# A wider third projection block, 34-row pairs in the last MLP step, and a written order for all engines

## The chip, the cores and the metric

The kernel runs on one core of one Trainium2 chip. The metric is the device time of one execution in microseconds. Before the change the median of three runs is 414.59 us (414.57 to 415.31). The profiled execution took 415.18 us; its span, from the first to the last instruction in the trace, is 413.4 us, at a mean granted TensorE clock of 0.999.

Names: TensorE (PE) multiplies matrices, its weight loads (PEld) run beside its matmuls; VectorE (DVE), ScalarE (ACT) and GpSimd (POOL) work element by element; SyncE (SP) issues the DMAs from one queue, in order.

## The reference

```python
S, D, F = 2048, 512, 1376
def _A_ref(x, wqkv, wo):            # H = 32 heads of 16, W = 8, dil = 2
    q, k, v = split(x @ wqkv)
    # token p attends to p, p-2, ..., p-14; places before 0 are masked
    logits = jnp.einsum("bhsd,bhswd->bhsw", q, kg) * scale
    attn = _softmax(logits, axis=-1)
    o = jnp.einsum("bhsw,bhswd->bhsd", attn, vg)
    return o.transpose(...).reshape(B, S, D) @ wo
def _B_ref(x, w1, b1, w2, b2):
    y = _layernorm(x, axis=-1)
    h = _gelu(jnp.einsum("bsd,df->bsf", y, w1) + b1)
    return jnp.einsum("bsf,fd->bsd", h, w2) + b2

xn = _layernorm(x, axis=-1)
return x + _A_ref(xn, A_wqkv, A_wo) * _silu(_B_ref(xn, B_w1, B_b1, B_w2, B_b2))
```

## The kernel before

**Arithmetic.** Every matmul of size is done three times in float16: an operand is split into a high part and a low remainder, and high x high, high x low and low x high are added in one PSUM bank. With D = 512 as KT = 4 blocks of 128 rows, one output tile takes 12 matmuls. The scales that keep the parts in float16's range come from sums of squares of the weights, worked out at the start (`sumsq`, L421; the results are `qsc`, `hsc`, `zsc`, `osc`).

**Tiling.** The 2048 tokens stand in two halves `c` (even and odd tokens) of NI = 8 tiles of 128. The 32 heads are NHB = 4 head blocks of 8 heads. The eight units u = (c, hb) each take `qkv`, then `attention`. The MLP runs over four chunks `ch` of 512 tokens and NF = 11 blocks of F: ten of 128 and a last one of FL = 96.

**The projection.** `qkv(c, hb, u)` multiplies each token tile's yT by 384 columns of `wq` (q, k and v of 8 heads; L746), evacuates with a scale to `U[u % 2]` on ScalarE (L763) or VectorE (L759), and copies the rows that neighbouring partitions need by DMA (L771). The first projection tiles wait for `prep` of the weights on ScalarE: squares with a running sum (`scale_q`, L514), high parts (`prep_q`, L536), and casts of the transposed, normalised tokens (`y0`, L687).

**Attention** is element work on VectorE (L805 to L863) and GpSimd (L873, L883); its result `o` (L848) is transposed by DMA (L851) to `oT`.

**The MLP.** `mlp1(ch, f)` makes 128 rows of h for 512 tokens in 12 matmuls (L1016), then a gelu (L1033) and the high part (L1036) on ScalarE and the low part (L1038) on VectorE. For f = 10 only 96 rows exist. `mlp2(ch, f)` follows two steps later (LAG = 2): 12 matmuls (L1052) into four banks z, one for each token tile, that collect all 11 blocks. The last block's h is in `hlast`, 96 rows and one row for the bias, so its 12 matmuls contract 97 rows. Then a silu, and the result g goes to DRAM (`gd`) until the end.

**The end.** `wo_first` (half c = 0) and `wo_last` (half c = 1, L951) multiply oT by `wo`; for half 1 VectorE evacuates with the product by g (L993), x is added on VectorE (L1000) or GpSimd (L997), and SP issues the output (L1002).

**The order.** Every operation is noted with its engine, a cost, what it reads and writes, and a priority. `Plan.issue` (L222) is a list scheduler: at each step it takes, over all engines, the ready operation that can start first by its cost model (`place`, L187), with the priority among those of an engine, and the program is issued in that order. Buffers of a ring are given out in the same step.

## Time and profile before

| what | value |
|---|---|
| median of three runs | 414.59 us |
| profiled execution | 415.18 us |
| its span | 413.4 us |
| granted TensorE clock | 0.999 |
| matmuls in the trace | 2083 |
| DMA moved | 46.41 MB, mean 112 GB/s |

The span can be cut in four. The columns are the length, and then the busy time of TensorE, weight loads, VectorE, ScalarE and GpSimd with their instructions in brackets, the granted clock, the share of the DMA engines and GB/s:

```profile
0.00:20.00 20.00, 16.48 (x81) 10.39 (x82) 14.00 (x44) 10.65 (x20) 11.55 (x21) 1.00 0.92 344
20.00:50.00 30.00, 29.73 (x179) 17.11 (x177) 25.86 (x50) 28.00 (x53) 9.77 (x7) 1.00 0.70 200
50.00:393.00 343.00, 342.96 (x1739) 170.54 (x1737) 329.05 (x273) 183.47 (x282) 95.20 (x101) 1.00 0.32 91
393.00:413.40 20.40, 16.76 (x90) 8.58 (x88) 10.61 (x16) 0.00 (x0) 3.82 (x3) 0.98 0.35 117
```

A group of instructions is read like this: line and engine, operation, output <- inputs (buffer numbers left out), partitions x elements, xcount | busy time in us, mean ns of one | idle time of the engine just before them, and what ended it. In the timeline the first two numbers are the start and the length in us, and a bracket at the end names the idle time before and its releaser. A record of a matmul is longer than the distance to the next, because matmuls overlap in the pipeline.

### The profile page before, as it was taken

Reading aid. Unit: us, or ns where it says so; the run is one execution under the profiler, and the core shown is the slowest. Engines: PE = TensorE matmul, PEld = TensorE weight load, DVE = VectorE, ACT = ScalarE, POOL = GpSimd, SP = SyncE. Lnnn points to the kernel's source line nnn. Section 1 sums busy time; section 2 is a strip of 40 time slices with the busy share of each in tenths; the row PEclk is TensorE's granted clock in tenths of the full one; section 3 lists DMA queues with packets and bytes.
Section 4 is the critical chain, followed back from the end, with each engine's and each line's share of the span. In section 5 each row is a group of like instructions: output and inputs, shape, how many; then the busy total and the mean of one; then the engine's idle time right before and its main releaser. Section 6 shows DMA issues by size and latency. Waiting matters only on the chain.

```text
span 413.4 us, 5554 instructions
## 1 busy us (share of the span) xinstructions
PE 405.9 (98%) x2083; PEld 206.6 (50%) x2083; DVE 379.5 (92%) x379; ACT 222.1 (54%) x353; POOL 120.3 (29%) x131
## 2 busy tenths in 40 slices
PE   8799999999999999999999999999999999999996
PEld 5555544445654455445544554455455544444443
DVE  4996989998999999989998999999999998999954
ACT  4699899994549655843384252225212393263500
POOL 3834002004380425042504330434033404520021
PEclk9999999999999999999999999999999999999999
DMA  8958717030045137720172034223604244007133
GB/s 281 397 112 258 235 61 230 0 128 1 1 142 152 28 93 183 149 46 2 48 221 75 0 102 116 68 86 88 205 7 122 88 111 145 0 18 238 23 102 131
DMA packets 47211, 46.41 MB, mean 112 GB/s; under 512 B 31785, under 2 KB 32225, under 8 KB 46673
## 3 DMA queue, kind: packets, MB, share of 16 engines
q1 hardware_dynamic: 47184, 46.06, 37.6%
q8 instruction: 16, 0.26, 0.3%
q14 instruction: 11, 0.08, 0.1%
HBM read 24.06 MB, written 7.34 MB: 76 GB/s over the span
## 4 chain that ended last, share of the span: by engine, by line
PE 92%; ACT 3%; issue 1%; DVE 1%; POOL 1%; ACTq 0%
PE z L1052 28%; PE ps L1016 28%; PE ps L746 25%; PE ps L929 5%; PE ps L961 2%; PE z L961 2%; PE pl L746 1%; ACT w L421 1%; PE pl L961 1%; ACT f L673 1%; ACT yT L687 0%; ACT wq L536 0%; POOL wq L471 0%; POOL rb L635 0%; ACT prod L661 0%
## 5 line engine op out<-in xcount | busy, mean ns | idle before, releaser
L1016 PE MATMUL ps<-yT,w 128*128 128x512 f16 (+1 forms) x528 | 120.4, 379 | 0.0
L746 PE MATMUL ps<-wq,yT 128*128 128x384 f16 x708 | 117.0, 326 | 0.2 <-DVE U L759 0.2
L1052 PE MATMUL z<-w,h 128*128 128x512 f16 x480 | 110.4, 379 | 0.0
L746 PEld LDWEIGHTS <-yT 128*128 128x128 f16 x744 | 72.5, 98 | 49.2 <-issue 1.0
L1016 PEld LDWEIGHTS <-w 128*128 128x128 f16 (+1 forms) x528 | 52.8, 100 | 61.0
L805 DVE TENSOR_TENSOR prod<-U 128x2048 f32<-128x2048 f32 x32 | 73.2, 2286 | 2.2 <-POOL prod L883 0.7
L1052 PEld LDWEIGHTS <-h 128*128 128x128 f16 x480 | 46.6, 98 | 55.5 <-issue 0.3
L808 DVE TENSOR_REDUCE L<-prod 128x128 f32<-128x2048 f32 x32 | 73.0, 2281 | 0.4
L1033 ACT ACTIVATE ps<-ps,b1T,hsc 128x512 f32<-128x512 f32 (+1 forms) x44 | 32.9, 748 | 73.4 <-PE ps L1016 72.2
L863 DVE TENSOR_TENSOR prod<-pl,U 128x2048 f32<-128x2048 f32 x28 | 63.2, 2283 | 4.2 <-POOL prod L873 4.1
L763 ACT ACTIVATE U<-ps,cs 128x384 f32<-128x384 f32 x54 | 31.2, 580 | 65.2 <-PE ps L746 65.2
L873 POOL TENSOR_TENSOR prod<-prod,prod 128x2048 f32<-128x2048 f32 x7 | 31.7, 4531 | 113.8 <-DVE prod L863 99.6
L883 POOL TENSOR_TENSOR prod<-prod 128x1024 f32<-128x1024 f32 x14 | 32.9, 2349 | 0.0
L882 POOL COPY gate<-prod 1x1 f32<-1x1 f32 x21 | 5.5, 264 | 91.0 <-DVE prod L805 82.2
L1038 DVE SCALAR_TENSOR_TENSOR h<-ps,hsc,h 128x512 f16<-128x512 f32 x40 | 29.6, 741 | 1.7 <-ACT h L1036 1.4
L1036 ACT ACTIVATE h<-ps,hsc 128x512 f16<-128x512 f32 x40 | 27.3, 684 | 1.3 <-PE z L1052 0.4
L929 PE MATMUL ps<-wo,oT 128*128 128x512 f16 x96 | 21.7, 379 | 0.0
L858 DVE TENSOR_TENSOR prod<-prod,prod 128x2048 f32<-128x2048 f32 x9 | 20.5, 2282 | 0.0
L1033 ACT ACT_TABLE_LOAD x10 | 12.8, 1283 | 8.6 <-PE ps L1016 8.5
L883 POOL TENSOR_TENSOR prod<-prod,prod 128x1024 f32<-128x1024 f32 x7 | 16.4, 2347 | 0.0
L961 PEld LDWEIGHTS <-oT 128*128 128x128 f16 x108 | 10.6, 98 | 10.4
L929 PEld LDWEIGHTS <-oT 128*128 128x128 f16 x96 | 9.4, 98 | 11.2
(179 smaller groups left out, 377.8 us busy)
## 6 DMA issues: line engine op xcount, KB each, us to landing
f<-in_A_x_dram SPq DMA_DIRECT2D x31, 256.0 KB, 3.5
U<-U SPq DMA_DIRECT2D x16, 392.0 KB, 4.0
gd<-f SPq DMA_DIRECT2D x12, 256.0 KB, 3.4
prod<-in_A_x_dram SPq DMA_DIRECT2D x8, 256.0 KB, 6.9
oT<-in_B_w_dram SPq DMA_DIRECT2D x2, 1024.0 KB
yT<-in_B_w_dram SPq DMA_DIRECT2D x2, 1024.0 KB, 7.9
f<-gd SPq DMA_DIRECT2D x8, 256.0 KB, 2.7
out_dram<-f SPq DMA_DIRECT2D x8, 256.0 KB, 2.8
```

The costliest lines, as they stand in the source:

```text
L746: nc.tensor.matmul(b.t[:, 0:384], y[:, s, k, o:o + P], wq[:, hb, t, k], start=(n == 0), stop=(n == 11))
L763: act(384, lambda i=i, b=b: nc.scalar.activation(U3[:, i:i + 31:15, :], b.t[:, 0:384].rearrange("p (t e) -> p t e", t=3), AF.Identity, sca ...
L805: dve(2048, lambda p2=p2, g=g: nc.vector.tensor_tensor(p2(), q, slots(Ut, KH, 2 * g), op=ALU.mult), qk + [("kh", ub, 0), ("kh", ub, 1), (" ...
L808: dve(2048, lambda pr=pr, g=g: nc.vector.tensor_reduce(L3()[:, 2 * g:2 * g + 2], pr.t.rearrange("p (r f d) -> p r f d", r=2, d=DH), AX.X, ...
L863: dve(2048, lambda: nc.vector.tensor_tensor(pr.t.rearrange("p (r f d) -> p r f d", r=2, d=DH), A3()[:, 2 * g:2 * g + 2].rearrange("p r (f ...
L873: pool(4.75, lambda: nc.gpsimd.tensor_tensor(acc.t, acc.t, p1.t, op=ALU.add), [acc, p1], [acc])
L883: nc.gpsimd.tensor_tensor(x.t[:, 0:1024], x.t[:, 0:1024], y(), op=ALU.add)
L929: nc.tensor.matmul(b.t, oT[:, hb, i // 4, s, i % 4], wo[:, t, hb], start=(hb == 0 and n == 0), stop=(hb == last and n == 2))
L961: nc.tensor.matmul(b.t[:, cols], oT[:, hb, i // 4, s, i % 4], wo[:, t, hb, cols], start=(start and hb == 0 and n == 0), stop=(stop and hb ...
L1016: nc.tensor.matmul(b.t[0:M], w1[:, s, f * 512 + k * M:f * 512 + (k + 1) * M], yT[ch][:, t, k], start=(n == 0), stop=(n == 11))
L1033: act(512, lambda: nc.scalar.activation(b.t[0:M], b.t[0:M], AF.Gelu_apprx_tanh, bias=b1T[0:M, f:f + 1], scale=hsc[0:M, 1:2]), [b, ("b1T",) ...
L1052: nc.tensor.matmul(z.t, hl[s][0:K, t * P:(t + 1) * P], w2[0:K, w, f], start=(f == 0 and n == 0), stop=(f == NF - 1 and n == 2))
```

## The change

Four things are changed.

1. **Third head block wider.** The block hb = 2 (HLAST) of `wq` gets 96 more columns: the last block of w1. So in the units (0, 2) and (1, 2) each of the 192 projection matmuls has 480 columns, and the last MLP1 block comes out with tokens in the partitions. ScalarE evacuates the 96 columns of each tile into `hl0` or `first`. For each chunk, `last_block` adds the bias on GpSimd, does the gelu and the high part on ScalarE (32 rows' worth of it twice), the low parts on VectorE, and transposes both parts by two DMAs. The 48 matmuls of 96 output rows, their gelus, high and low parts are gone.
2. **Last MLP2 step packed.** The 96 rows of the high part and 32 rows of remainder fill 128 rows; two such matmuls for each token tile (high and low part of w2), and a third with the 34 rows that are left (32 and two rows of bias), two token tiles side by side on partitions 0 to 33 and 64 to 97, each into its own bank. w2 gets two more blocks in the input for this (`w2t`, block 11 and 12), loaded by two more DMAs and prepared on ScalarE and VectorE.
3. **Order from a table.** `ORDER` lists the numbers of all 1262 operations; `issue` takes them in this order, and a ring's slots are given out by it. Some costs of the planner are changed too (GpSimd's, the DMA rate).
4. **Room.** `ident` and `mean1` lie in a tile `first` that is used again for the packed block; the row of v for the halo is kept in DRAM; two rings are smaller (mx 4 to 2, cs 8 to 7); `wq` is one tile for each head block.

By number of matmuls: 744 of 384 columns become 552, and 192 of 480 columns are new; 48 of 96 x 512 and 48 of 97 rows go, 32 full ones and 16 of 34 rows come. VectorE's list grows from 375 to 385 rows, ScalarE's table loads from 25 to 26, SP's list by 8 transposes and 2 loads.

```diff
+HLAST = 2
+ORDER = (
+    0, 1, 19, 2, 115, 130, 132, 129, 128, 114, 117, 120, 133, 124, 131, 121, 116, 111, 119, 20, 113, 21, 112,
...
+)
@@ issue
-        order = []
+        order, fixed = [], [self.ops[n] for n in reversed(ORDER)]
         while len(order) < len(self.ops):
             best = None
-            for e, cand in engs.items():
+            if fixed:
+                o = fixed.pop()
+                t = max([self.earliest(o)] + [min(b.ring.free) for b in o.bufs if b.slot is None])
+                assert not o.npred and t < float("inf")
+                best = (t, o)
+            for e, cand in engs.items() if best is None else ():
...
-                    b.ring.free[b.slot] = b.end
+                    b.ring.free[b.slot] = len(order) if ORDER else b.end
@@ tile_mixer
-    wq = sb.tile([P, NHB, 2, KT, 384], F16, name="wq")
-    w1 = sb.tile([P, 2, KT * F], F16, name="w1")
+    wq = [sb.tile([P, 2, KT, 384 + FL * (hb == HLAST)], F16, name=f"wq{hb}") for hb in range(NHB)]
+    w1 = sb.tile([P, 2, W1C[3]], F16, name="w1")
+    wl = wq[HLAST][:, :, :, 384:384 + FL]
@@ new function
+    def last_block(ch):
+        n = 4 * FL
+        h16 = R_f.new()
...
+        with prio(PEV):
+            pool(1.0, lambda: nc.gpsimd.tensor_tensor(x3(), x3(), row, op=ALU.add), xk + [("b1T",)], xk)
+            act(n, lambda: nc.scalar.activation(x, x, AF.Gelu_apprx_tanh), xk, xk,
+                aps=1, table="gelu")
+            act(2 * n, lambda: nc.scalar.activation(
+                v()[:, :, :, 0:FL], x.rearrange("p (t o f) -> p t o f", t=4, o=1).to_broadcast([P, 4, 2, FL]),
+                AF.Identity, scale=hsc[:, 2:3]), xk + [("hsc2",)], [(h16, 0)])
...
@@ qkv
-                    nc.tensor.matmul(b.t[:, 0:384], y[:, s, k, o:o + P], wq[:, hb, t, k],
+                    nc.tensor.matmul(b.t[:, 0:wide], y[:, s, k, o:o + P], wq[hb][:, t, k],
...
+            if hb == HLAST:
+                act(FL, lambda i=i, b=b: nc.scalar.activation(
+                    hpt[i // 4][:, (i % 4) * FL:(i % 4 + 1) * FL], b.t[:, 384:384 + FL], AF.Identity, scale=hsc[:, 1:2]),
...
+        for j in range(2 if hb == HLAST else 0):
+            last_block(2 * c + j)
@@ mlp2
+        for a in range(0, 4, 2) if f == NF - 1 else ():
+            def pair(a=a, z=list(zt)):
+                ha = hlt[ch % 2].rearrange("p a (t x) -> p (a t) x", t=4)
+                for t in range(a, a + 2):
+                    for w in range(2):
+                        nc.tensor.matmul(z[t].t, ha[:, 2 * t + w], w2[:, w, f], start=False, stop=False)
+                for t in range(a, a + 2):
+                    r = slice(64 * (t - a), 64 * (t - a) + FR + 2)
+                    nc.tensor.matmul(z[t].t, hlc[ch % 2][r, a // 2], w2t[r], start=False, stop=True)
```

**ScalarE at the start.** `wq` is the projection's weights, `prod` and `U` the places where they arrive, `z` the PSUM bank of a transposed tile, `rb` a normalisation factor, `oT` the place of a quarter of w1. Before:

```order
L514 ACTIVATE wq,s_122<-prod_93 128x768 x2
L536 ACTIVATE wq<-prod_93,qsc 128x384 x4
L514 ACTIVATE wq,s_124<-U_87 128x768
L687 CAST yT_82<-z_146 128x4x128
L514 ACTIVATE wq,s_124<-U_87 128x768
L659 ACTIVATE rb_151<-pb_150,rb_151 128x1
L661 ACTIVATE prod_95<-prod_95,rb_151 128x512
```

and in the changed kernel:

```order
L597 ACTIVATE wq_82,s_125<-prod_100 128x768 x2
L597 ACTIVATE wq_83,s_126<-U_94 128x768
L619 ACTIVATE wq_82<-prod_100,qsc 128x384 x3
L597 ACTIVATE wq_83,s_126<-U_94 128x768
L619 ACTIVATE wq_82<-prod_100,qsc 128x384
L770 CAST yT_89<-z_150 128x4x128
L742 ACTIVATE rb_155<-pb_154,rb_155 128x1
L744 ACTIVATE prod_101<-prod_101,rb_155 128x512
L504 ACTIVATE w_86,s_129<-oT 128x2048
L619 ACTIVATE wq_83<-U_94,qsc 128x768
L770 CAST yT_89<-z_150 128x4x128
```

Both squares over the second block (from `U`) now stand ahead of the first cast, and the square over the quarter of w1 (L504) ahead of the second cast; before, it stood behind it.

**TensorE at the last MLP2 step of the first chunk.** `z00` to `z30` are the four banks. Before:

```order
L1052 LDWEIGHTS hlast_91
L1052 MATMUL z00_143<-w2_80,hlast_91 128x512
L1052 LDWEIGHTS hlast_91
L1052 MATMUL z00_143<-w2_80,hlast_91 128x512
L1052 LDWEIGHTS hlast_91
L1052 MATMUL z00_143<-w2_80,hlast_91 128x512
```

and in the changed kernel, with `hl0` the packed block and `tail` the 34-row operands:

```order
L1172 LDWEIGHTS hl0_98
L1172 MATMUL z20_149<-w2_87,hl0_98 128x512
L1172 LDWEIGHTS hl0_98
L1172 MATMUL z20_149<-w2_87,hl0_98 128x512
L1172 LDWEIGHTS hl0_98
L1172 MATMUL z30_150<-w2_87,hl0_98 128x512
L1172 LDWEIGHTS hl0_98
L1172 MATMUL z30_150<-w2_87,hl0_98 128x512
L1175 LDWEIGHTS tail_78
L1175 MATMUL z20_149<-tail_78 128x512
L1175 LDWEIGHTS tail_78
L1175 MATMUL z30_150<-tail_78 128x512
```

Three matmuls a bank become two full ones and one half of a pair.

**SP's queue at the end.** Before, each output waits for its own addition, and the last is that of the last tile:

```order
L1002 DMA out_0_dram<-U0_86 128x512 [waits DMAHW3_49,DVE_49]
L1002 DMA out_0_dram<-U0_86 128x512 [waits DMAHW4_49,DVE_49]
L1002 DMA out_0_dram<-U0_86 128x256 [waits DMAHW5_49,DVE_49]
L1002 DMA out_0_dram<-U0_86 128x256 [waits DMAHW6_49,DVE_49]
```

and in the changed kernel:

```order
L1127 DMA out_0_dram<-U0_93 128x512 [waits DMAHW3_49]
L1127 DMA out_0_dram<-U0_93 128x512 [waits DMAHW4_49,DVE_49]
L1127 DMA out_0_dram<-U0_93 128x512 [waits DMAHW5_49]
L1048 DMA out_0_dram<-f5_108 128x512 [waits DMAHW6_49]
L1127 DMA out_0_dram<-U0_93 128x512 [waits DMAHW7_49]
L1127 DMA out_0_dram<-U0_93 128x256 [waits DMAHW0_49]
```

The second row waits for the last addition on VectorE (z20's tile, whose matmuls are the last on TensorE), and four outputs that wait for no engine come behind it; one of them (L1048) is an output of half 0.

More of the change, by code (lines that the diff above doesn't have):

```diff
@@ L383, in tile_mixer @@
     cT = sb.tile([P, DIL, NI], F32, name="cT")
-    b1T = sb.tile([P, NF], F32, name="b1T")
-    hlast = sb.tile([P, 2, 512], F16, name="hlast")
+    b1T = sb.tile([P, NF + FL], F32, name="b1T")
+    hl0 = sb.tile([P, 512], F32, name="hl0")
+    hpt = [hl0[:, 0:512], first[:, 0:512]]
+    hlt = [h.bitcast(F16).rearrange("p (a t) -> p a t", a=2) for h in hpt]
     gd = dr.tile([DIL, NI, P, D], F32, name="gd")
@@ L1008, in mlp1 @@
     def mlp1(ch, f):
-        M = P if f < NF - 1 else FL
+        M = P
         c, j = ch // 2, ch % 2
@@ L1024, in mlp1 @@
                after=pl.users([b]))
-        if f < NF - 1:
-            h = R_h.new()
-            hi, lo = (lambda: h.t[:, 0]), (lambda: h.t[:, 1])
-        else:
-            h = ("hlast",)
-            hi, lo = (lambda: hlast[:, 0]), (lambda: hlast[:, 1])
-        hk = (h, 0) if f < NF - 1 else ("hlast", 0)
+        h = R_h.new()
+        hi, lo = (lambda: h.t[:, 0]), (lambda: h.t[:, 1])
+        hk = (h, 0)
         with prio(PR_H + pl.prio * 1e-6):
@@ L1051, in mm @@
                 for n, (s, w) in enumerate(((0, 0), (0, 1), (1, 0))):
-                    nc.tensor.matmul(z.t, hl[s][0:K, t * P:(t + 1) * P], w2[0:K, w, f],
-                                     start=(f == 0 and n == 0), stop=(f == NF - 1 and n == 2))
-            pe(3, 512, mm, [h, hk, w2key[f]] + ([("hrow",)] if f == NF - 1 else []), [zt[t]])
+                    nc.tensor.matmul(z.t, hl[s][:, t * P:(t + 1) * P], w2[:, w, f],
+                                     start=(f == 0 and n == 0), stop=False)
+            pe(3, 512, mm, [h, hk, w2key[f]], [zt[t]])
         if f < NF - 1:
@@ L1224, in tile_mixer @@
     col5 = R_s.new()
-    dve(5, lambda: nc.vector.memset(col5.t[:, 0:5], 0.0), [], [(col5, k) for k in range(5)], port=False)
+    dve(6, lambda: nc.vector.memset(col5.t[:, 0:6], 0.0), [], [(col5, k) for k in range(6)], port=False)
     for h in range(2):
```

143 lines of the change are left out of this document (101 added, 42 removed), and 61 rows, old and new, of the table ORDER.

## The prediction

> **What bounds the kernel now.** I read the page first, then the chain of waits, then TensorE's groups by shape, and last the timeline at both ends.
>
> ```profile
> span 413.4 us, 5554 instructions
> PE 405.9 (98%) x2083; PEld 206.6 (50%) x2083; DVE 379.5 (92%) x379; ACT 222.1 (54%) x353; POOL 120.3 (29%) x131
> PE 92%; ACT 3%; issue 1%; DVE 1%; POOL 1%; ACTq 0%
> ...
> 50.00:100.00 50.00, 50.00 (x240) 23.01 (x238) 46.64 (x54) 44.09 (x85) 6.92 (x9) 1.00 0.29 94
> 100.00:150.00 50.00, 49.96 (x265) 25.70 (x264) 48.80 (x48) 30.05 (x46) 17.50 (x16) 1.00 0.30 83
> 350.00:400.00 50.00, 50.00 (x233) 23.03 (x232) 44.45 (x37) 19.32 (x25) 9.63 (x14) 1.00 0.23 64
> ```
>
> TensorE holds 92% of the chain. In the three 50 us windows (length; then busy time of PE, weight load, VectorE, ScalarE, GpSimd; granted clock; DMA share) it has no gap at all, at a granted clock of 1.00. So in the body one matmul less is time saved, and everything else costs only if TensorE has to wait for it. The span has 413.4 − 405.9 = 7.5 us without TensorE, all of it at the ends. I count the sum against this execution, 415.18 us for a span of 413.4 us, and carry the difference over to the median of the three runs, 414.59 us, which lies 0.6 us below it.
>
> **TensorE: wide block for narrow matmuls.** The price of a matmul is the distance from start to start, since records overlap:
>
> ```profile
> 308.49 15.76 PE L746 MATMUL ps<-wq,yT 128*128 128x384 f16 x96
> 324.09 2.75 PE L1052 MATMUL z<-w,h 128*128 128x512 f16 x12
> 326.68 2.75 PE L1016 MATMUL ps<-yT,w 128*128 128x512 f16 x12
> ...
> L746 PE MATMUL ps<-wq,yT 128*128 128x384 f16 x708 | 117.0, 326 | 0.2 <-DVE U L759 0.2
> L1016 PE MATMUL ps<-yT,w 128*128 128x512 f16 x480 | 109.3, 379 | 0.0
> L1052 PE MATMUL z<-w,hlast 97*128 97x512 f16 x48 | 11.0, 379 | 0.0
> L1016 PE MATMUL ps<-yT,w 128*96 128x512 f16 x48 | 11.0, 379 | 0.0
> ```
>
> 384 columns: (324.09 − 308.49)/96 = 0.1625 us. 512 columns: (326.68 − 324.09)/12 = 0.2158 us. The slope is 0.0533/128 = 0.000416 us a column, so 96 more columns cost 0.040 us. A matmul with 97 rows or 96 output rows takes the same 379 ns as a full one: its unused part is paid for. The change drops 48 matmuls of the 96-row form, 48 x 0.2158 = −10.36 us, and makes 192 wider, 192 x 0.040 = +7.68 us. **Term 1: −2.7 us.** It rests on the slope holding from 384 to 480 columns, which lies between two measured widths.
>
> **TensorE: the last MLP2 step.** 48 matmuls of 97 rows become 32 full ones and 16 of 34 rows, in 8 pairs, one of a pair on rows 0 to 33 and one on rows 64 to 97, into different banks. If the two run at once, 8 x 0.2158 = −1.73 us. No row shows two matmuls at once or a matmul with such a shape. The nearest row is the 97-row form: it follows full ones at the ordinary distance (idle 0.0), so a change of rows alone costs nothing there. What a pair could give back is the weight load of its second member:
>
> ```profile
> L1052 PEld LDWEIGHTS <-h 128*128 128x128 f16 x480 | 46.6, 98 | 55.5 <-issue 0.3
> ```
>
> 8 x 0.098 = 0.78 us, if no matmul lies beside it. That leaves −0.95 us; between −1.73 and −0.95 I take the middle. **Term 2: −1.3 us.** The other end: the pair runs one after the other and TensorE empties at every change of the layout. What emptying costs is what a record is longer than its distance, 379 − 216 = 163 ns; 16 changes (into and out of each pair) make 2.6 us. With the gain of running at once kept, 2.6 − 1.7 = +0.9 us; with 16 bare weight loads on top, 0.9 + 1.6 = +2.5 us.
>
> The Trainium skill, "TensorEngine Tiling (Array Packing)", Key Properties under Tiling Modes, says two things here: different tiles can load weights and multiply in parallel, and changing the tiling mode drains the TensorE. By the first the sum would have −1.73, by the second +0.9; no row here shows either.
>
> **The tail.** This is where the changed order costs most. Last matmul, its eviction, the addition and the output now:
>
> ```profile
> 407.18 0.75 DVE L993 SCALAR_TENSOR_TENSOR U<-z,osc,U 128x512 f32<-128x512 f32 x1 [1.11 <-PE z L961]
> 407.97 0.69 DVE L1000 TENSOR_TENSOR U<-U,f 128x512 f32<-128x512 f32 x1
> 408.29 1.47 PE L961 MATMUL ps<-wo,oT 128*128 128x256 f16 x12
> 409.80 0.48 DVE L993 SCALAR_TENSOR_TENSOR U<-ps,osc,U 128x256 f32<-128x256 f32 x1 [0.29 <-PE ps L961]
> 410.32 0.42 DVE L1000 TENSOR_TENSOR U<-U 128x256 f32<-128x256 f32 x1
> ...
> 400.91 1.48 SPq L1002 DMA_DIRECT2D out_dram<-U  x3
> 410.77 0.33 SPq L1002 DMA_DIRECT2D out_dram<-U  x1
> ...
> out_dram<-U SPq DMA_DIRECT2D x2, 128.0 KB, 1.7
> ```
>
> Call E the end of the last matmul, 408.29 + 1.47 = 409.76. Now one output of 256 columns is issued at E + 1.01 and lands 1.7 us later, at 412.47; the span ends 0.93 us behind that, E + 3.64. In the changed order the last matmuls are the last three of a 512-wide tile. Behind them VectorE does its 512-wide eviction, a 256-wide addition and the 512-wide addition. From 407.18 to 408.66 the eviction and its addition take 1.48 us; with 0.42 between them and the delay of about 0.05, that output is issued at E + 1.95. Four others, ready long before, stand behind it on SP's queue. Three issues spanned 1.48 us, the last 0.33 of it its own, so the spacing is 1.15/2 = 0.575 us, if none of these waited for data; without that it is 0.33. The last issue comes 4 x 0.575 = 2.3 us later, or 4 x 0.33 = 1.3 us, lands after 1.7, and the span ends at E + 6.9 or E + 5.9. Against E + 3.64 that is +3.2 or +2.3. **Term 3: +2.8 us**, the middle; its whole cost would vanish only if the outputs were issued in the order in which they are ready.
>
> **The front.** TensorE's own waits before the body, and ScalarE around them:
>
> ```profile
> 12.86 0.66 PE L683 MATMUL z<-ident,prod 128*128 128x128 f32 x4 [1.65 <-POOL prod L665]
> 17.84 1.85 PE L683 MATMUL z<-ident,prod 128*128 128x128 f32 x12 [0.40 <-DVE prod L668]
> 19.54 4.71 PE L746 MATMUL ps<-wq,yT 128*128 128x384 f16 x28
> 24.44 5.36 PE L746 MATMUL ps<-wq,yT 128*128 128x384 f16 x32 [0.19 <-DVE U L759]
> ...
> 13.55 0.59 ACT L687 CAST yT<-z 128x512 f16<-128x512 f32 x1 [1.67 <-PE z L683]
> 14.03 0.85 ACT L514 ACTIVATE wq<-U 128x768 bf16<-128x768 f32 x1
> 17.86 0.28 ACT L659 ACTIVATE rb<-pb,rb 128x1 f32<-128x1 f32 x1
> 18.18 0.81 ACT L661 ACTIVATE prod<-prod,rb 128x512 f32<-128x512 f32 x1
> 20.24 1.05 ACT L687 CAST yT<-z 128x512 f16<-128x512 f32 x2
> 22.02 1.90 ACT L421 ACTIVATE w<-oT 128x2048 bf16<-128x2048 f32 x1
> ```
>
> The square of the second projection block (0.85) is moved ahead of the last part of the first block's weights and of the first transposed tile's cast. Its cover is the 1.67 us that ScalarE idles there. The square over a quarter of w1 (1.90) is moved ahead of the next cast. Against it two rows of 0.28 + 0.81, of another tile's scaling, move behind that cast; counted along ScalarE that cast comes about 0.5 us later, and TensorE has 28 projection matmuls (19.54 to 24.25) ready beside it. Bounds: −2.05 us if both of TensorE's waits, 1.65 and 0.40, go, and +1.9 us if the second square has no cover. **Term 4: 0.**
>
> **The body.** What is new off TensorE, for each of four chunks of 512 tokens: four evictions of 96 columns on ScalarE, a 384-wide bias addition on GpSimd, one gelu and one cast on ScalarE, two small subtractions on VectorE, and two transposes on SP's queue. What goes: gelu, cast and subtraction of the 96-row step.
>
> ```profile
> L1036 ACT ACTIVATE h<-ps,hsc 128x512 f16<-128x512 f32 x40 | 27.3, 684 | 1.3 <-PE z L1052 0.4
> L1038 DVE SCALAR_TENSOR_TENSOR hlast<-ps,hsc,hlast 96x512 f16<-96x512 f32 x4 | 3.0, 744 | 1.9 <-ACT hlast L1036 1.9
> L1000 DVE TENSOR_TENSOR U<-U 128x256 f32<-128x256 f32 x2 | 0.8, 424 | 0.1
> DVE prod L863 <- POOL prod L873: 4.1, 3, 1.9
> 392.97 0.75 DVE L848 SCALAR_TENSOR_TENSOR o<-prod,osc,o 128x512 f16<-128x512 f32 x1 [0.79 <-ACT o L846]
> 396.62 2.10 PE L961 MATMUL ps<-wo,oT 128*128 128x512 f16 x9
> yT<-f SPq DMA_TRANSPOSE x12, 3.3
> ```
>
> VectorE loses 3.0 us and gets 4 x 0.42 for the subtractions of 256 elements, less for the 128-wide ones (0.28 each, an estimate on the line through the rows of 512 and 256), and two operations of some 0.7 us on the packed w2 rows: −3.0 + 1.7 + 1.1 + 1.4 = +1.2 us. That is hidden: its attention is done at 393.7, TensorE's matmuls that need its last head block start at 396.62, and one wait for GpSimd alone was 4.1 us in three. ScalarE is 54% busy. What can be late is a chunk's own packed block: its two transposes (3.3 us each from issue to landing) stand behind whatever waits on SP's queue, and TensorE's four z banks wait for them. In the first and third chunk I count 3 to 8 us from the subtractions to the first matmul that reads the transposed block. If the first were too late by its whole 3.3 us, +3 us. **Term 5: +0.3 us** (0 to 3).
>
> **Sum:** −2.7 − 1.3 + 2.8 + 0 + 0.3 = −0.9 us, so a span of 412.5 us and a median of 414.59 − 0.9 = **413.7 us**.
>
> **Rivals.**
>
> B, *the outputs' queue is no loss*: if issues to queues that are ready take less than the spacing I read, or the last tile's addition comes before the other outputs hold it up, term 3 goes: −0.9 − 2.8 = −3.7, 410.9 us. For it: those outputs' data are long ready. Against it: one queue, issued in order, in every SP row of the trace. It decides if the last output is issued within 1.3 us of E.
>
> C, *ScalarE's front becomes the bound*: both moved squares lie on the path to the casts, 0.85 + 1.90 = 2.75 us, so −0.9 + 2.75 = +1.85, 416.4 us, slower than before. For it: 3% of the chain already runs over ScalarE, all of it here, and TensorE has little else ready before 30 us. Against it: 1.67 us idle ahead of the first cast, and 28 projection matmuls beside the second. It decides when the cast of the second group of tiles ends after TensorE has used up those matmuls, 24.25 us on the present clock. A late transpose of a packed block (up to +3 us) would end at a like time.
>
> D, *the pairs cost more than they save*: TensorE empties into and out of each pair: +0.9 in place of −1.3, so −0.9 + 2.2 = +1.3, 415.9 us; with bare weight loads 417.5 us. For it: the layout does change 16 times, and each record is 163 ns longer than its distance. Against it: the 97-row form shows no loss. It decides from a start-to-start time of 0.14 us more than 0.2158 per change. By the skill's sentence on draining this is the outcome; the trace of before cannot tell.
>
> **How the numbers follow.** A change under 0.2% (0.83 us, 413.76 to 415.42) could not be told from none. The sum as forecast: 0.48, with a range of its own of 412.3 to 415.3 us, from term 3's 2.3 to 3.2, term 2's 0.8 and some of terms 4 and 5; of it 0.24 is faster, 0.18 within 0.2%, 0.06 slower. B 0.16, faster. C 0.22 and D 0.14, slower. Together faster 0.40, same 0.18, slower 0.42: the single likeliest time lies just on the faster side, while two mechanisms that I could not close lie on the other. The range goes from B's 410.9 to D's worst, 417.5; outside are half of B (with a gain at the front too) and two mishaps at once, about 0.16.
>
> **What would show it.** Term 1: 480-wide matmuls 0.2025 us apart (0.1625 + 0.040), and none with 96 output rows. Term 2: the two records of a pair start less than 0.1 us apart, and the distance from the full matmul before a pair to the one after it is about 0.43 us (two slots); 0.65 us or more says D. Term 3: five outputs issued after the last addition, and the span ending 6 to 7 us behind the last matmul. Term 4: TensorE's idle time before 30 us about as now. Term 5: no wait of TensorE between 50 and 390 us of over 0.5 us, above all none for a transpose. The forecast is wrong if TensorE's idle time in the body is over 2 us, or if the tail costs under 1 us.

## The result, and the profile after

| | before | changed |
|---|---|---|
| median of the runs | 414.58 us (4 runs, 414.49 to 415.31) | 417.75 us (4 runs, 417.27 to 418.01) |
| profiled execution | 415.18 us | 418.01 us |
| its span | 413.4 us | 416.2 us |
| end of the last matmul in the span | 409.76 us | 408.87 us |
| from there to the end of the span | 3.64 us | 7.33 us |

The changed kernel is slower, ratio 1.0071 with a 95% interval of 1.0054 to 1.0089. The forecast was 413.7 us in a range of 410.9 to 417.5: the sign was wrong, and the time lies just above the range. How large the loss is varies: the same kernel, run again beside the kernel before on two other chips, was 1.9 and 2.7 us slower (section "The front").

The page of the changed kernel, the span, the engines' busy time and the chain of waits:

```profile
span 416.2 us, 5499 instructions
PE 404.3 (97%) x2035; PEld 199.9 (48%) x2035; DVE 383.4 (92%) x386; ACT 227.8 (55%) x374; POOL 134.3 (32%) x134
PE 93%; DVE 3%; ACT 1%; DMA 1%; issue 0%; DVEq 0%
```

TensorE is still the chain. It has 1.6 us less to do, and 416.2 − 404.3 = 11.9 us without work in place of 7.5. Three of the four windows, with the columns as shown for the kernel before (length; busy time of TensorE, weight loads, VectorE, ScalarE, GpSimd; clock; DMA):

```profile
0.00:20.00 20.00, 16.37 (x72) 10.05 (x73) 13.08 (x43) 11.43 (x20) 10.84 (x20) 1.00 0.92 343
...
50.00:393.00 343.00, 342.28 (x1702) 164.48 (x1700) 328.40 (x274) 185.25 (x296) 111.25 (x106) 1.00 0.36 93
393.00:416.20 23.20, 15.87 (x86) 7.97 (x84) 14.26 (x20) 2.45 (x4) 4.59 (x3) 0.93 0.47 155
```

The body has one hole, 343.00 − 342.28 = 0.72 us, and the last window the long tail. TensorE's timeline at the places where the change lies (start, length, and in brackets the wait before):

```profile
119.02 2.75 PE L1141 MATMUL ps<-yT,w 128*128 128x512 f16 x12 [0.72 <-DVE h L1159]
...
130.03 1.03 PE L1172 MATMUL z<-w,hl 128*128 128x512 f16 x4
130.98 0.39 PE L1175 MATMUL z<-tail 34*128 34x512 f16 x2
131.31 1.04 PE L1172 MATMUL z<-w,hl 128*128 128x512 f16 x4
132.28 0.39 PE L1175 MATMUL z<-tail 34*128 34x512 f16 x2
132.60 2.76 PE L1141 MATMUL ps<-yT,w 128*128 128x512 f16 x12
...
269.40 2.59 PE L864 MATMUL ps<-wq,yT 128*128 128x480 f16 x12
271.83 2.75 PE L1054 MATMUL ps<-wo,oT 128*128 128x512 f16 x12
```

480 columns take (271.83 − 269.40)/12 = 0.2025 us, as forecast to the digit. The two matmuls of a pair fill 0.39 us together, and one record alone is 387 ns long: they do run at once. But four full matmuls should bring the pair 4 x 0.2158 = 0.863 us after 130.03; it comes after 0.95, and the next full one starts 0.33 us behind the pair. The whole step, 130.03 to 132.60, takes 2.57 us. Twelve ordinary slots are 2.59.

The end, on SP's queue and on VectorE and TensorE:

```profile
407.35 4.09 SPq L1127 DMA_DIRECT2D out_dram<-U  x7
408.06 0.81 PE L1086 MATMUL z<-wo,oT 128*128 128x512 f16 x3
409.91 0.68 DVE L1125 TENSOR_TENSOR U<-U,f 128x512 f32<-128x512 f32 x1
411.50 0.45 SPq L1048 DMA_DIRECT2D out_dram<-f  x1
411.99 1.16 SPq L1127 DMA_DIRECT2D out_dram<-U  x2
```

Not one output leaves before 407.35, and the last of the ten is issued at about 413.15 − 0.33 = 412.82, when the last addition has been done since 410.59.

**The account of the 2.8 us** between the two spans, from the two traces: −2.76 for the wide block and the pairs (term 1 and 4 x (2.57 − 2.59)); +0.72 for the wait at 119 us; +3.69 for the tail (7.33 − 3.64). What is left is 2.8 + 2.76 − 0.72 − 3.69 = about +1.1 us, and it lies ahead of 50 us.

### The profile page after: what moved, and what is told of

Its sections match the earlier page's. It is cut to its first block, busy times and chain, and to the rows that moved or that the text cites. A ratio compares the mean times of both kernels' runs of the same rounds, so it can differ in the third digit from the quotient of the medians.

```text
span 416.2 us, 5499 instructions
## 1 busy us (share of the span) xinstructions
PE 404.3 (97%) x2035; PEld 199.9 (48%) x2035; DVE 383.4 (92%) x386; ACT 227.8 (55%) x374; POOL 134.3 (32%) x134
## 4 chain that ended last, share of the span: by engine, by line
PE 93%; DVE 3%; ACT 1%; DMA 1%; issue 0%; DVEq 0%
PE ps L864 28%; PE ps L1141 25%; PE z L1184 24%; PE ps L1054 5%; PE ps L1086 2%; PE z L1086 2%; PE z L1172 2%; PE pl L864 1%; PE pl L700 1%; DMA U<-in_A_xt_dram 1%; PE pl L1086 1%; PE z L1175 1%; DVE lw L651 1%; DVE L L933 0%; DVE bn L659 0%
## 5 line engine op out<-in xcount | busy, mean ns | idle before, releaser
L864 PE MATMUL ps<-wq,yT 128*128 128x384 f16 (+1 forms) x708 | 128.5, 337 | 0.2 <-ACT yT L770 0.2
L1141 PE MATMUL ps<-yT,w 128*128 128x512 f16 x480 | 109.5, 379 | 0.7 <-DVE h L1159 0.7
L1141 PEld LDWEIGHTS <-w 128*128 128x128 f16 x480 | 46.6, 98 | 56.4 <-issue 1.7
L998 POOL TENSOR_TENSOR prod<-prod,prod 128x2048 f32<-128x2048 f32 x7 | 40.3, 5757 | 88.2 <-DVE prod L988 88.2
L1154 ACT ACTIVATE ps<-ps,b1T,hsc 128x512 f32<-128x512 f32 x40 | 29.6, 748 | 30.6 <-PE ps L1141 29.6
L1159 DVE SCALAR_TENSOR_TENSOR h<-ps,hsc,h 128x512 f16<-128x512 f32 x40 | 29.7, 744 | 3.2 <-ACT h L1157 3.1
L1122 POOL TENSOR_TENSOR U<-U,f 128x512 f32<-128x512 f32 x3 | 4.6, 1542 | 34.8 <-DVE U L1118 34.8
```

Of the source, the lines that this page charges most:

```text
L864: nc.tensor.matmul(b.t[:, 0:wide], y[:, s, k, o:o + P], wq[hb][:, t, k], start=(n == 0), stop=(n == 11))
L998: pool(4.75, lambda: nc.gpsimd.tensor_tensor(acc.t, acc.t, p1.t, op=ALU.add), [acc, p1], [acc])
L1141: nc.tensor.matmul(b.t[0:M], w1[:, s, f * 512 + k * M:f * 512 + (k + 1) * M], yT[ch][:, t, k], start=(n == 0), stop=(n == 11))
L1159: dve(512, lambda: nc.vector.scalar_tensor_tensor(lo()[0:M], b.t[0:M], hsc[0:M, 2:3], hi()[0:M], op0=ALU.mult, op1=ALU.subtract), [b, hk], ...
```

## The experiments

In the table `ORDER` an operation is a number, so most edits move numbers. Line numbers in their profiles are some lines smaller than in the changed kernel, since the table is shorter.

### The outputs of the end

Only SP's numbers at the end of the table are moved (926 is the output of half 0, 1167 the last transpose, 1238 the load of an x tile, the rest are outputs):

```diff
-    1167, 1238, 1257, 1232, 1222, 1242, 1247, 1252, 1237, 926, 1227, 1261,
+    926, 1167, 1238, 1227, 1232, 1237, 1222, 1247, 1257, 1242, 1261, 1252,
```

> The order table alone is edited: SP issues the outputs of the end in the order in which their data are ready (the output of half 0 before the last transpose, then as the additions end), all else stays. Theory Q (the outputs stand behind one that is not ready, in one queue): the last output goes out at the end of the last addition, about 410.65 us in the changed kernel's trace, lands after 1.7 to 2.0 us and the span ends about 413.4, 2.8 us less than 416.2; the tail behind the last matmul falls from 7.33 to 4.5 us. Rival T (the transfers of the end are bound by their rate, so the order does not matter): less than 1 us saved.

Measured: 414.74 us against 414.77 us for the kernel before on the same chip, ratio 1.0002 (0.9992 to 1.0011); span 412.8 us. SP's queue and TensorE's last matmuls in that run:

```profile
402.03 8.06 SPq L1122 DMA_DIRECT2D out_dram<-U  x9
...
407.20 0.81 PE L1081 MATMUL z<-wo,oT 128*128 128x512 f16 x3
```

The outputs now start at 402.03, 5.3 us earlier (0.9 of it because this whole execution is earlier), and the tail is 412.8 − 408.01 = 4.79 us and not 7.33: −2.54 us by the order of ten DMA issues. Theory Q holds. The tail is still 1.15 us longer than before the change: the last issue, at 410.09 − 0.33 = 409.76, is followed by 3.04 us and not 2.63, and it comes 1.75 us after the last matmul and not 1.01, since VectorE now does a 512-wide eviction, a 256-wide and a 512-wide addition there, where it did a 256-wide eviction and addition. Why the landing takes longer was not tried.

### The wait at 119 us

```diff
-    ..., 520, 525, 304, 342, 577, ...
+    ..., 577, 520, 525, 304, 342, ...
```

577 is the subtraction (L1159) that frees TensorE's bank, 520 the reduction ahead of it.

> The order table alone is edited: one VectorE subtraction (the low part of a hidden block, the one that TensorE waited 0.72 us for at 119.0 us) stands ahead of the 2.28 us reduction before it and not behind it. Theory D (a plain matter of order on VectorE): TensorE's wait at 119 us goes and the span is 0.7 us shorter. Rival G (it was late because GpSimd held VectorE up, the 128x8 product of 2.16 us ahead of it, and so VectorE's whole chain is late): the wait moves to a later place and less than 0.3 us is saved.

Measured: 416.19 us, ratio 1.0031 (1.0019 to 1.0043) to the kernel before. TensorE at that place:

```profile
115.28 2.11 PE L1179 MATMUL z<-w,h 128*128 128x512 f16 x9
117.22 2.75 PE L1136 MATMUL ps<-yT,w 128*128 128x512 f16 x12
```

The two groups follow each other without a gap, and no other wait of the body took its place. Theory D holds for the place and the 0.7 us. What made the moment tight can be read in the changed kernel's trace, on VectorE and GpSimd:

```profile
113.49 2.16 DVE L651 TENSOR_TENSOR lw<-lw,mv 128x8 f32<-128x8 f32 x1
115.77 2.28 DVE L933 TENSOR_REDUCE L<-prod 128x128 f32<-128x2048 f32 x1
118.23 0.74 DVE L1159 SCALAR_TENSOR_TENSOR h<-ps,hsc,h 128x512 f16<-128x512 f32 x1
...
113.28 2.34 POOL L1008 TENSOR_TENSOR prod<-prod,prod 128x1024 f32<-128x1024 f32 x1
```

A product of 8 elements in a row lasts as long as GpSimd's product of 1024 beside it; before the change the same product took 0.17 us:

```profile
116.25 0.17 DVE L568 TENSOR_TENSOR lw<-lw,mv 128x8 f32<-128x8 f32 x1
```

That GpSimd holds it up is read from the two ends, 115.65 and 115.62, and was not tried by itself.

### The pairs

Two experiments. In the first, the full matmuls of the step come first and both pairs after them, in the first three chunks (in the table, 769 moves next to 770, so that the two halves of the step stand together in chunk 1):

```diff
-                for t in range(a, a + 2):
-                    r = slice(64 * (t - a), 64 * (t - a) + FR + 2)
-                    nc.tensor.matmul(z[t].t, hlc[ch % 2][r, a // 2], w2t[r], start=False, stop=True)
+                first = 0 if ch == 1 else 2
+                for b in [a] if ch == 3 else [] if a == first else [first, a]:
+                    for t in range(b, b + 2):
+                        r = slice(64 * (t - b), 64 * (t - b) + FR + 2)
+                        nc.tensor.matmul(z[t].t, hlc[ch % 2][r, b // 2], w2t[r], start=False, stop=True)
```

> In chunks 0, 1 and 2 the eight full matmuls of the last MLP2 step come first and then the two pairs one behind the other; so the layout of TensorE changes 2 times in a chunk and not 4. Theory W (each change of layout costs about 0.105 us, read off the changed kernel: from the last full matmul to the pair 0.30 us and from the pair to the next full one 0.32 us, where 0.216 is the ordinary distance): 3 x 2 x 0.105 = 0.63 us less, and the second pair starts 0.22 us behind the first. Rival L (each of these small matmuls has its own uncovered weight load): no change.

Measured: 418.41 us, ratio 1.0093 (1.0078 to 1.0107) to the kernel before, so no gain. In the trace, chunk 0 and chunk 1:

```profile
129.29 1.89 PE L1167 MATMUL z<-w,hl 128*128 128x512 f16 x8
131.11 0.60 PE L1172 MATMUL z<-tail 34*128 34x512 f16 x4
131.65 2.76 PE L1136 MATMUL ps<-yT,w 128*128 128x512 f16 x12
...
213.89 0.61 PE L1172 MATMUL z<-tail 34*128 34x512 f16 x4
216.11 2.75 PE L1136 MATMUL ps<-yT,w 128*128 128x512 f16 x12 [1.61 <-ACT U L877]
```

Where it stands well, the step takes 131.65 − 129.29 = 2.36 us in place of 2.57: two changes of layout less save 0.21 us, 0.105 each, as theory W says. Chunk 2 shows the same, 341.63 − 339.27 = 2.36 us. What the 0.105 us consist of, emptying or a weight load with no matmul beside it, these runs do not separate. In chunk 1 the edit had its own cost: the silu of two banks then came late, on ScalarE the evacuation of a projection bank stood behind it, and TensorE waited 1.61 us for that.

In the second, the small matmuls run one after the other over 98 rows of the whole array (each bank then gets the last 34 rows of both token tiles, so the kernel's result is another one, and only its time is of use):

```diff
-                    r = slice(64 * (t - a), 64 * (t - a) + FR + 2)
+                    r = slice(0, FR + 66)
```

> The pairs are undone in one respect: the two small matmuls of a pair contract rows 0 to 97 on the whole array, one after the other (each bank then gets the last 34 rows of both token tiles: that part of the computation is changed). No change of layout is left. Theory W (a pair gains one slot of 0.216 us and loses two changes of 0.105 us, so the packing is worth nothing): each full-full-small group takes 12 slots of 0.216 a chunk, 2.59 us against 2.57 with the pairs, and the time is the same within 0.2 us. Rival P (the pairs are worth the 1.3 us of the forecast): 1.3 us slower. Rival D (the changes of layout cost more than the pairs gain): 0.9 us faster or more.

```profile
129.90 1.03 PE L1167 MATMUL z<-w,hl 128*128 128x512 f16 x4
130.77 0.60 PE L1170 MATMUL z<-tail 98*128 98x512 f16 x2
...
132.50 2.75 PE L1136 MATMUL ps<-yT,w 128*128 128x512 f16 x12
```

The step is 132.50 − 129.90 = 2.60 us, 0.03 more than with the pairs, so packing them in the order that the change has is worth 0.1 us over four chunks. The times alone don't say it as well: 418.00 us (416.67 to 418.33) against 416.98 for the unaltered kernel on the same chip (416.66 to 417.61, next section but one); in the two profiled executions the last matmul ends 0.94 us apart, and that difference is in the front, in a part that the edit does not touch.

### The order table as a whole

```diff
-ORDER = (
-    0, 1, 19, 2, 115, ...
-)
+ORDER = ()
```

> The order table is emptied, so the planner's list scheduling sets the order as in the kernel before; the wider third block, the pairs and everything else stay. Theory O (the parts of the change are worth 2.7 us on TensorE and the table loses 2.5 us at the end and 0.7 us at 119 us): 414 to 415 us, with a tail behind the last matmul of 3.6 to 4.5 us. Rival B (list scheduling does not find room for the new work, and the table's order is the better one in the body): slower than the changed kernel, with waits of TensorE of over 3 us in the body.

Measured: 421.98 us, ratio 1.0163. Where its time goes is read from a second run of the same kernel:

> The kernel without the order table once more, since the profiled execution of e6 was a disturbed one: where its 4 to 5 us over the changed kernel lie. Theory B (list scheduling leaves TensorE waiting in the body for the new work): waits of TensorE of over 3 us between 50 and 390 us, named in the profile. Rival: the loss lies in the front and the tail.

421.71 us, ratio 1.0164 (1.0145 to 1.0182). TensorE there, and the same sum over w2 in the kernel before:

```profile
62.54 0.17 PE L455 MATMUL z<-s,fours 128*128 128x6 bf16 x1
67.05 0.59 PE L1121 MATMUL z<-w,h 128*128 128x512 f16 x1 [4.34 <-ACT w L502]
69.39 10.36 PE L1121 MATMUL z<-w,h 128*128 128x512 f16 x41 [1.75 <-DVE w L506]
```
```profile
56.58 0.17 PE L435 MATMUL z<-s,fours 128*128 128x5 bf16 x1
```

Theory O falls, and rival B holds. The parts of the change without the table lose 6.1 us at the first MLP2 step: the sum of squares over w2, now with a sixth column, is done at 62.5 us and not at 56.6, and w2's high parts are made only after it. Behind the second wait the 41 matmuls take 10.36/41 = 0.25 us each and not 0.216, at a granted clock of 0.89 between 70 and 80 us. So the table is not the loser of this change as a whole; it keeps TensorE fed between 50 and 390 us but for 0.72 us, and loses at the very end. The tail without it is 419.4 − 415.57 = 3.8 us.

### The front

The first theory was the order of the first operations. Two prefixes of the order of the kernel before were put in:

```diff
-    0, 1, 19, 2, 115, 130, 132, 129, 128, 114, 117, 120, 133, 124, 131, 121, 116, 111, 119, 20, 113, 21, 112,
...
+    the first 200 (120) operations as the kernel before orders them, the others as in the table
```

> The order table alone is edited: the first 200 operations stand in the order that the kernel before has (all engines, up to about 36 us), the rest as in the changed kernel. Theory F (the front's order delays the projection, mostly the sum of squares behind fill-in matmuls and the transposes ahead of the first projection matmuls): the first projection matmul starts at about 16.0 us in place of 18.5, the wait of 1.9 us goes, and the span is 1.2 us shorter. Rival S (the shared tiles or the smaller rings cause it, not the order): no change within 0.3 us, first projection matmul still after 18 us.

> The front again, with the order of the kernel before for the first 120 operations only (up to about 20 us). With 200 the front was early (first projection at 15.8 us) but VectorE met a wait of TensorE of 3.3 us at 45 us, where the two orders meet. Theory F (the order of the first 20 us alone is late, about 1.2 us): the first projection matmul at 15.8 us, no wait of over 1 us between 20 and 60 us, and 1.0 to 1.5 us less than the changed kernel of this call. Rival M (the two orders do not fit together at any seam): the first projection is early and a wait of 1 us or more appears between 20 and 60 us.

Measured: 422.2 us with 200 (no unaltered run beside it), 417.70 us with 120 (the changed kernel on the same chip: 416.98). TensorE's longest wait in the body with 200, and then with 120 (us in all, times, longest):

```profile
PE ps L859 <- DVE U L873: 3.5, 2, 3.3
```
```profile
PE ps L859 <- ACT U L877: 1.3, 2, 0.9
```

The first projection matmul did come early, at 15.77 and 15.95 us where the changed kernel has 18.51, and it was no use: the time came back as waits of 3.3 and 1.3 us where the two orders meet. Theory F falls, since neither is faster. Rival M holds with 200; with 120 the longest single wait is 0.9 us, just short of its mark. Because of these waits the two runs do not say what the order of the front costs by itself; the next runs do.

The unaltered changed kernel, run again on two other chips:

> The changed kernel once more, unaltered, as the measure for the others of this call. Its profiled execution reached every place of the body some 0.9 us later than the profiled executions of the experiments with an edited end did, with nothing edited ahead of it. Theory V (the front varies from execution to execution by up to 1 us, with the first loads): median 417.0 to 417.8, and a span of 415.3 to 416.3. Rival: 416.2 again within 0.2 us, and then the edits of the tail had an effect on the front.

> The changed kernel once more, as the measure for this call. Theory H (in some of its executions TensorE runs at half its speed until about 9.5 us, in others until about 6 us, and this decides 0.9 us of the front): times in two groups near 416.8 and 417.8.

416.98 us (416.66 to 417.61) and 417.64 us (416.44 to 418.20), where the kernel before has 415.09 and 414.94 us. The times are spread and do not fall into the two groups of theory H. The float32 matmuls at 6 to 9 us in the first profiled execution of the changed kernel, and in the second (`k0_again`):

```profile
6.18 1.65 PE L700 MATMUL pl<-prod,U 128*128 128x384 f32 x2 [0.35 <-DVE U L693]
7.62 0.64 PE L1303 MATMUL z<-first,fours 128*128 128x256 bf16 x2
8.05 1.49 PE L700 MATMUL pl<-prod,U 128*128 128x384 f32 x2
```
```profile
6.18 0.91 PE L695 MATMUL pl<-prod,U 128*128 128x384 f32 x2 [0.35 <-DVE U L688]
6.93 0.38 PE L1298 MATMUL z<-first,fours 128*128 128x256 bf16 x2
...
407.06 0.81 PE L1081 MATMUL z<-wo,oT 128*128 128x512 f16 x3
```

The same matmuls in the same program take 7.62 − 6.18 = 1.44 us for two in one execution and 6.93 − 6.18 = 0.75 in the other. In the first TensorE works at half its speed until about 9.5 us; all that follows is about 1 us later: the first projection matmul starts at 18.51 us in the first execution and at 17.52 us in the second. In the second the last matmul ends at 407.87: against 409.76 before, that is −1.89, where −2.76 + 0.72 = −2.04 is due. So in this execution, with TensorE at full speed from 6 us on, the front costs 0.15 us, although the first projection matmul is 1.56 us later than before (15.96 us). The third profiled execution (`k1_again`, 417.48 us) is fast from 6 us on too, but there a load of x holds TensorE up for 0.84 us and not 0.37, and the last matmul ends at 408.36: by the same sum its front costs 0.64 us. So both the speed and the first loads vary, as theories H and V say in turn.

The Trainium skill, "TensorE: Matmul & The Clock Gate", Part 1, says that the array runs at half its clock until it has been busy for a window of some 3.4 us, and that this window runs freely, so that the moment differs from execution to execution. The two executions agree with both: the half, and a different moment in the same program.

Two fill-in matmuls were moved into the gap ahead of 6.18 us:

```diff
-    20, 113, 21, 112, 22, 122, 127, 23,
+    20, 113, 21, 112, 122, 127, 22, 23,
```

> The order table alone is edited: two of the fill-in matmuls stand ahead of the first float32 matmul of 384 columns, where TensorE was idle for 0.35 us (four fill-in matmuls there as in the kernel before, and not two). Theory H (the gaps at 5 to 6 us delay the moment when TensorE gets its full speed): the float32 matmuls between 6 and 9 us take about 510 ns and not 890 in every execution, all times lie in the lower group, near 416.8. Rival W (whether TensorE is fast by 6 us does not depend on this gap): two groups of times as in the kernel unaltered.

Measured 417.19 us (416.38 to 418.43), against 417.64 for the unaltered kernel on the same chip: not told apart, and single times still 2 us apart, so theory H falls as far as this gap should decide the time. Its profiled execution (418.43) was fast at 6 us and slow later:

```profile
16.45 0.95 PE L761 MATMUL z<-first,prod 128*128 128x128 f32 x4 [1.90 <-ACT prod L739]
...
18.48 1.49 PE L859 MATMUL ps<-wq,yT 128*128 128x384 f16 x4
19.76 0.76 PE L761 MATMUL z<-first,prod 128*128 128x128 f32 x4
```

Behind the idle 1.90 us four matmuls of 384 columns take (19.76 − 18.48)/4 = 0.32 us each, twice 0.1625, and the column of the granted clock shows it: 0.67 between 16 and 18 us, 0.50 between 18 and 20. So half speed can come back behind a second gap, and the fill at the first is not enough. The gap alone does not decide it: in `k0_again` the same 1.9 us stand ahead of 16.38 us, and the four matmuls behind it are 0.1625 us apart. This gap is shorter than the window of 3.4 us that the same page of the Trainium skill gives for falling back; here the measurement stands.

### Versions that put it together

Three edits at once, the outputs, the subtraction and the pairs side by side where it did no harm:

```diff
-    1167, 1238, 1257, 1232, 1222, 1242, 1247, 1252, 1237, 926, 1227, 1261,
+    926, 1167, 1238, 1227, 1232, 1237, 1222, 1247, 1257, 1242, 1261, 1252,
-    ..., 520, 525, 304, 342, 577, ...
+    ..., 577, 520, 525, 304, 342, ...
-                for t in range(a, a + 2):
+                for b in [a] if ch % 2 else [] if a == 2 else [2, 0]:
```

> Three edits together: the outputs in the order in which they are ready, the VectorE subtraction ahead of the reduction, and the pairs side by side in chunks 0 and 2 alone (in chunk 1 it had made a silu late and with it a bank, 1.6 us). Theory (the costs stand one behind the other on TensorE and on SP's queue, so they add): 2.5 + 0.7 + 0.4 = 3.6 us less than the changed kernel of this call, about the time of the kernel before or 0.5 us below. Rival (VectorE's chain binds behind TensorE, so what TensorE gains in the body returns as a wait): 2.5 us less only.

413.64 us against 416.98 for the changed kernel and 415.09 for the kernel before, on the same chip, ratio to the latter 0.9965 (0.9950 to 0.9979). 3.34 of the 3.6 us are there: the costs add.

With the fill-in matmuls and another end:

```diff
-    20, 113, 21, 112, 22, 122, 127, 23,
+    20, 113, 21, 112, 122, 127, 22, 23,
-    1258, 1249, 1259, 1250, 1260, 1251,
+    1249, 1258, 1250, 1251, 1259, 1260,
```

(1249 to 1251 are the matmuls, the eviction and the addition of the last 512-wide tile, 1258 to 1260 those of the 256-wide one; the last two outputs change places as well.)

> The three edits of e8 (outputs in order of readiness, the subtraction ahead of the reduction, pairs side by side in chunks 0 and 2), the fill-in matmuls of e10, and at the very end the 256-wide tile after the 512-wide one on TensorE, VectorE and SP. Theory: the front in its faster form always (413.0), and 0.4 us less at the end, since a 256-wide eviction and addition follow the last matmul and not a 512-wide one with another ahead of it: 412.4 to 412.9 us. Rival: as e8, 413.6, in two groups.

> The kernel of e11 once more, unaltered, as the measure for this call: 413.0 to 413.6, with single times up to 414.8.

413.29 and 413.40 us, ratios 0.9960 and 0.9969 to the kernel before beside them: against 0.9965 of e8 the difference is inside the scatter. The 0.4 us at the end are not there: from the last matmul to the end of the span e11 takes 412.2 − 407.31 = 4.89 us, e8 411.2 − 406.43 = 4.77. The front is not always in its faster form either: in the profiled executions of both runs the matmuls behind the 1.9 us run at half speed again. Then the front once more, now the gap of 1.9 us itself:

```diff
-ScalarE: ..., 45, 169, 47, 51, 58, 177, 173, 60, ...
+ScalarE: ..., 45, 47, 51, 169, 58, 177, 173, 60, ...
-TensorE: ..., 30, 171, 110, 59, 31, 138, 73, 139, ...
+TensorE: ..., 30, 31, 171, 110, 138, 59, 139, 73, ...
```

> e11 with the order at the front edited: on ScalarE the last part of the first block's weights and the first cast stand ahead of the second square over U, and on TensorE the first projection matmuls stand ahead of the transposes of the next tile, where TensorE sat idle for 1.9 us at 15 us. Theory G (the front's loss and its scatter are this gap: TensorE's clock falls to a half in and behind it in some executions): the gap falls below 1 us, no execution has matmuls of 384 columns at 0.32 us distance behind 16 us, times 412.4 to 412.9 with a spread under 1 us. Rival L (what follows waits for the low parts of the weights anyway, about 19.5 us): the gap is only moved, the time stays within 0.3 us of k2.

> e12 and, on ScalarE, the second cast ahead of the square over the quarter of w1 (1.9 us), as the kernel before has it. Theory C (the square in front of the cast costs the 0.5 us that the walk along ScalarE gave): 0.3 to 0.6 us less than e12. Rival (term 4 was right that it is hidden): within 0.2 us of e12, or slower because the sum over w1 comes later.

```profile
15.28 0.81 PE L859 MATMUL ps<-wq,yT 128*128 128x384 f16 x4
16.70 0.66 PE L761 MATMUL z<-first,prod 128*128 128x128 f32 x4 [0.60 <-ACT prod L739]
17.20 0.81 PE L859 MATMUL ps<-wq,yT 128*128 128x384 f16 x4
17.84 0.60 PE L761 MATMUL z<-first,prod 128*128 128x128 f32 x4
19.89 4.07 PE L859 MATMUL ps<-wq,yT 128*128 128x384 f16 x24 [1.44 <-ACT yT L765]
```

The lines are e12's. It has 413.05 us (412.37 to 413.29), ratio 0.9951 (0.9937 to 0.9964) to the kernel before; k2 on the same chip 413.40 (412.59 to 414.76), 0.9969 (0.9958 to 0.9981). The gap is cut to 0.60 us, but 1.44 us come back at 18.4 us, so the median moves by 0.35 us, near the 0.3 of rival L. The high times are missing: four of k2's ten runs are 414.0 us or more, and they are the four with a mean granted clock of 0.996, where the other six have 1.000; e12's five have 0.998 or 0.999. That fits theory G, as far as the scatter goes, and five runs are too few to prove it. e13, 413.42, is no faster than e12: the square ahead of the second cast costs nothing that its removal would give back. e12 has the lowest median here, 1.8 us below the kernel before on the same chip; from e11, k2 and e13 it is not told apart.

## Why the prediction was wrong, point by point

**Term 1, −2.7 us, right.** 480 columns take 0.2025 us.

**Term 2, −1.3 us, wrong: about −0.1.** The step that failed is the choice between −1.73 and −0.95 by the row of 97 rows, "so a change of rows alone costs nothing there". A change of the layout is another thing than a shorter contraction. Running at once gains one slot of 0.216 us a pair, and each of the two changes costs 0.105 us. Rival D had the mechanism; its price of 163 ns was too high, so its +0.9 us did not come either. The trace agrees with both sentences of the Trainium skill's "TensorEngine Tiling (Array Packing)", Key Properties: the pair runs in parallel, and the change of mode costs time. Only the two together give the answer, and it needed the measured price.

**Term 3, +2.8 us, right in the mechanism, too small: +3.7.** "Four others, ready long before, stand behind it" was right, and rival B's condition (last issue within 1.3 us of the last matmul's end) failed with 412.82 − 408.87 = 3.95 us. What was missed is the head of the queue: the first output in it waits for an addition that ends at 407.3, so all ten leave in 5.8 us. The span ends 3.38 us behind the last issue, where it was 2.63 before; whether the ten crowd each other there was not tried. The issue itself came sooner than forecast (3.95 and not 4.25 us after the last matmul); the landing was mis-sized. That it is the order, and not the amount, e1 shows with −2.54 us.

**Term 4, 0, right as a matter of order, wrong as a time.** With TensorE at full speed from 6 us on the front costs 0.15 us in one execution and 0.64 in another. In the profiled execution of the result it was about 1.1 us, because TensorE stayed at half speed until 9.5 us. What decides the moment stays open; in the same program it differs from execution to execution. The step that failed is that the prediction counted waits alone, and half speed is no wait: TensorE reads as busy. The waits themselves came as forecast: 1.89, 0.35 and 0.15 us before 30 us, where they were 1.65, 0.40 and 0.19. Rival C did not come true. The first projection matmul is 2.5 us later and the wait of 1.89 us is one for ScalarE, but ScalarE's scaling there has first waited 0.57 us for VectorE, with the moved square already done; and e12 and e13, with the first and then both squares moved back, gain 0.35 us at most.

**Term 5, +0.3 us, too small: +0.72.** The step that failed is "That is hidden", drawn from VectorE's spare time over the whole body and at its end. One subtraction stood behind a reduction of 2.28 us that it did not need, with 0.7 us too little room. The place that was feared, the transposes of the packed block, brought no wait at all.

**The sum.** −0.9 was forecast, +2.8 came in the profiled execution: 1.2 from term 2, 0.9 from term 3, 1.1 from term 4, 0.4 from term 5, together 3.6 of the 3.7. All four errors lie on the side of slower. For terms 2 and 3 the mechanism of the loss was named, and the middle of a range was taken; term 5 was set near the low end of its range on spare time as a sum; half speed in the front was not named at all. About 1 us of the error depends on the execution: on the chip where the changed kernel took 416.98 us it lies inside the range, and is still 1.9 us slower than the kernel before there.

## What to carry to other kernels

In a queue that issues in order, sort the last outputs by when their data are ready: here ten DMA issues in another order were worth 2.5 us, nearly all that the arithmetic saved (2.7 us). A saving of whole matmul slots by packing has to be charged with the change of layout on both sides; put packed matmuls one behind the other, so that one change serves several pairs. Spare time of an engine as a sum says nothing about one operation that another engine waits for: look at what stands ahead of that operation.

## What the runs showed of the hardware that was not expected

A change between full matmuls and the pair layout costs about 0.105 us each way, and within the layout two pairs follow at the ordinary 0.216 us (2.36 us for the step of e3).

TensorE's speed in the first 20 us differs between executions of one program: 1.44 us or 0.75 us for the same two float32 matmuls, 0.32 or 0.1625 us for a matmul of 384 columns behind a gap of 1.9 us. For the first of these the column of the granted clock reads 1.00 from 0 to 20 us, so only the distance of the matmuls shows it. The second stands in the column too, 0.50 between 18 and 20 us in e10.

A product of 8 elements in a row on VectorE took 2.16 us and ended with GpSimd's product beside it, where the same product took 0.17 us in the kernel before.
